# Seven block products instead of eight for w_out in the last three batches, with the relu kept in fp32

## The chip, the cores and the metric

The kernel runs on one core of a Trainium2 chip. The metric is the device time of one execution in microseconds (us). A profile of one execution stands beside it; engines are PE (TensorE; PEld is its weight load), DVE (VectorE), ACT (ScalarE), POOL (GpSimd) and SP (SyncE, which here issues DMAs).

## The reference

Block-sparse attention with a sorting network, then an FFN with a squared relu, for 4 batches, 8 heads, 768 positions of 64 elements:

```python
P = sort_net                                  # (4, 8, 8, 8), normalised by rows and columns, five times
k_sorted = einsum('bhij,bhjcd->bhicd', P, k_b)    # 8 blocks of 96 positions; v likewise
scores = scale * matmul(q_b, k_sb.T)              # inside a block
attn = softmax(scores)
x = matmul(attn, v_sb)  ->  (3072, 512)
h = maximum(x @ w_in, 0)                          # (3072, 2048)
out = (h * h) @ w_out                             # (3072, 512)
```

## The kernel before, in words

The FFN works on groups of 384 tokens, two to a batch. Its input stands transposed in `xT` (128 x 4 x 3072, bf16). An *up* is one of 16 slices of d_ff: four matmuls with 384 columns into a PSUM bank (`hp`, L1010). ACT takes the relu out of the bank into a bf16 tile `h1` (L1018), DVE squares it into `h2` (L1021), which holds the 16 slices of a group. A *down* is one tile of 128 tokens: 16 matmuls of 512 columns into a bank (`op`, L1040) with slices of `h2` as weights and `w_out_bf` as moving operand, in four parts of four. ACT or DVE copies the bank to `ob`, and SP stores it (L989). The last tile of all is done in two pieces of 384 and 128 columns (`last_tile`, L1068). Ups and downs share three banks (`psf`); attention has four banks in two pairs (`p2`) and one of its own (`ps1`).

Attention works on pairs of heads (hp 0 to 3). For batches 2 and 3 its steps are: N and V (`s_nat`, L780) multiply k and v by the sorting matrix on PE, in small tiles of the array; ACT or DVE takes the result out (`kn`, `vn`). Z (`s_turn`) turns k and q: SP issues a DMA transpose from `kn` to `kx` (L835), DVE copies that into `kvT` (L840); DVE copies q into `qi` (L852), and a DMA transpose brings it to `qz` (L862). S (`s_sc`, L695) makes the scores with row-tiled matmuls, ACT the exps (L724). A (`s_av`, L886) averages v, DVE divides (`rec` L896, `ao` L897). X (`s_xt`) turns the result into `xT`, by DMA transpose (L921), or, for hp 3 of batches 0 and 1, by PE (L939) and a copy. q of batch 1 is turned by PE (`s_q`, L574).

The order of the work is set at build time. Each step is recorded with a cost, its engine or engines and what it depends on; `Plan.run` walks through them like a list scheduler and fixes the order on every engine. PE has two queues, attention and FFN, and the table DUES says behind how many FFN pieces an attention step is due. On the chip each engine runs its instructions in that order and waits on semaphores. POOL issues the loads of q, k and v; those of a late batch stand behind a small copy (`held`, L1156) that waits for x^T of the batch before.

Of the kernel before, what the change touches and what calls it, by code (L numbers as in the profile page):

```python
# [8 lines left out]
FP32 = mybir.dt.float32  # L9
# [30 lines left out]
    (2, "A"): (86.0, 88.0, 99.0, 94.5),  # L40
    (2, "X"): (97.5, 103.0, 103.0, 102.0),
    (3, "L"): (109.0,),
    (3, "N"): (111.5, 130.0),
# [4 lines left out]
    (3, "X"): (150.5, 170.0, 236.5, 211.5),
# [5 lines left out]
         "F4 F6 F7 X3")  # L54


class Op:


    def __init__(self, eng, cost, fn, deps, due=0, mode="full"):  # L60
# [47 lines left out]
class Plan:  # L108
# [27 lines left out]
    def run(self):  # L136
# [4 lines left out]
        while att or ffn or rest:  # L141
            best = None
            for op in rest:
# [5 lines left out]
                if best is None or s < best[0][0]:  # L149
                    best = ((s, s + c), op, e, c)  # L150
# [34 lines left out]
def kernel(  # L185
# [92 lines left out]
    kvT_r, et_r, vs_r, qz_r = [], [], [], []  # L278
    for n in range(3):
# [41 lines left out]
    w_t = const.tile([128, NH // 4, 4, NB], BF16)  # L321
    qkv = {}
# [23 lines left out]
    def load(b, t, h0, n, p=slice(0, 128), deps=()):  # L346
        def dst_src():
# [6 lines left out]
            readers[b - 2] + [holds[b]] if b > 1 else list(deps),  # L354
# [90 lines left out]
    tiles = {}  # L445

# [378 lines left out]
    def q_late(z):  # L825
        return qz_r[z % 3][:, z // 3, :, :]
# [390 lines left out]
```

## Time and profile before

| | us |
|---|---|
| median of 3 runs | 217.51 (217.35 to 217.57) |
| span of the profiled execution, first to last instruction | 215.8 |
| what lies outside the span, if that execution took the median | 1.7 |
| PE busy | 209.8 |
| ACT busy | 122.4 |
| DVE busy | 110.0 |
| POOL busy | 27.0 |

The profiled execution's own time is shown by its span alone; its sum with what lies around it is set against the median. In a group's row stand the line, engine and operation, output<-input, shapes and count, then busy us, mean ns of one, and the idle time ahead of them with what ended it. Matmuls are pipelined, so the mean of one is longer than the spacing. A chain row has its start, its length and what ran.

### The profile page before, as it was taken

To read this page: it belongs to the slowest core of one execution; us is meant where nothing else is said; L and a number is where in the kernel's file an instruction comes from. 1 tells how busy PE (TensorE), PEld (TensorE's weight loads), DVE (VectorE), ACT (ScalarE), POOL (GpSimd) and SP (SyncE) were. 2 spreads that over 40 slices of the span, in tenths; PEclk is the share of its full clock that TensorE was granted. 3 is DMA by queue.
4 is the path that set the end of the run, shared out by engine and by line. 5 is a ranking of instruction groups with operands and counts; after the bars stand their busy time and mean duration, and the time that the engine had idled before them with its cause. 6 is when DMAs were issued, how large, how long until landed. Compare 5 with 4: busy or idle time off the path is not lost.

```text
span 215.8 us, 5098 instructions
## 1 busy us (share of the span) xinstructions
PE 209.8 (97%) x2036; PEld 115.7 (54%) x2036; DVE 110.0 (51%) x316; ACT 122.4 (57%) x251; POOL 27.0 (13%) x47
## 2 busy tenths in 40 slices
PE   7899999999999999999999999999999999999994
PEld 2477675446654565445655465445655555455542
DVE  5877677146795446335875047407775154015300
ACT  4787985248765277347774278318874375137421
POOL 7983230000000700000000420000000000000000
PEclk9999999999999999999999999999999999999999
DMA  6999999999978599199994699497988410231012
GB/s 151 216 202 207 207 207 207 191 225 274 185 160 107 94 229 213 24 195 220 169 197 118 114 195 212 90 211 165 163 204 115 103 45 3 49 73 24 0 52 97
DMA packets 47959, 31.91 MB, mean 148 GB/s; under 512 B 27392, under 2 KB 43008, under 8 KB 47936
## 3 DMA queue, kind: packets, MB, share of 16 engines
q1 hardware_dynamic: 35712, 18.35, 41.2%
q0 software_dynamic: 12224, 13.24, 37.1%
q8 instruction: 16, 0.26, 0.5%
q14 instruction: 7, 0.06, 0.1%
HBM read 29.70 MB, written 8.72 MB: 178 GB/s over the span
## 4 chain that ended last, share of the span: by engine, by line
PE 94%; DMA 2%; ACT 1%; issue 1%; DVE 0%; POOLq 0%
PE hp L1010 39%; PE op L1040 37%; PE p L886 4%; PE p L695 4%; DMA qb<-in_q_dram 2%; PE p L451 2%; PE p L780 2%; PE op L1068 2%; PE qtp L574 1%; PE vbp L744 1%; PE tp L624 1%; PE p L660 1%; PE hp L966 0%; PE xtp L939 0%; ACT et L715 0%
## 5 line engine op out<-in xcount | busy, mean ns | idle before, releaser
L1010 PE MATMUL hp<-xT,w_in_bf 128*128 128x384 bf16 x506 | 87.6, 326 | 0.0
L1040 PE MATMUL op<-w_out_bf,h 128*128 128x512 bf16 x368 | 84.9, 379 | 0.0
L1021 DVE TENSOR_TENSOR h<-h 128x384 bf16<-128x384 bf16 x128 | 44.0, 355 | 56.1 <-ACT h L1018 55.5
L1018 ACT ACTIVATE h<-hp 128x384 bf16<-128x384 f32 x128 | 61.8, 495 | 17.6 <-PE hp L1010 14.8
L1010 PEld LDWEIGHTS <-w_in_bf 128*128 128x128 bf16 x506 | 47.7, 98 | 32.2 <-issue 1.1
L1040 PEld LDWEIGHTS <-h 128*128 128x128 bf16 x368 | 33.9, 98 | 37.9 <-issue 1.0
L248 ACT COPY ob<-op 128x512 f32<-128x512 f32 (+2 forms) x25 | 14.2, 569 | 49.0 <-PE op L1040 46.6
L724 ACT ACTIVATE et<-p 96x384 bf16<-96x384 f32 x48 | 19.9, 487 | 6.1 <-PE p L695 6.1
L897 DVE TENSOR_TENSOR ao<-p,rec 96x512 bf16<-96x512 f32 x32 | 22.0, 686 | 1.3 <-DVE rec L896 0.2
L886 PEld LDWEIGHTS <-et 96*128 96x128 bf16 x256 | 11.2, 97 | 5.3 <-issue 0.7
L896 DVE RECIPROCAL rec<-p 96x8 f32<-96x8 f32 x32 | 6.4, 201 | 10.6 <-PE p L886 10.2
L1156 POOL COPY held<-xT 1x3 bf16<-1x3 bf16 (+1 forms) x2 | 0.4, 184 | 84.6 <-DMA xT<-ao 84.6
L250 DVE CAST vn<-p 128x768 bf16<-128x768 f32 x6 | 5.7, 958 | 7.3 <-PE p L780 7.2
L250 DVE CAST kn<-p 128x768 bf16<-128x768 f32 x5 | 4.8, 958 | 9.1 <-PE p L780 9.1
L886 PE MATMUL p<-vblk,et 96*128 96x65 bf16 x192 | 9.4, 193 | 0.0
L451 PE MATMUL p<-ones 128*128 128x512 bf16 (+1 forms) x28 | 8.2, 439 | 1.1 <-DVE ones L274 1.1
L695 PEld LDWEIGHTS <-kvT 64*128 64x128 bf16 x256 | 6.1, 94 | 5.3 <-issue 3.4
L840 DVE COPY kvT<-kx 128x768 bf16<-128x768 bf16 x10 | 8.5, 848 | 0.0
L248 ACT CAST vn<-p 128x768 bf16<-128x768 f32 x6 | 4.8, 797 | 5.8 <-PE p L780 5.8
L330 POOL DMA_DIRECT2D kb<-in_k_dram x10 | 6.5, 649 | 4.4 <-DMA w_in_bf<-in_moe_w_in_dram 1.8
L330 POOL DMA_DIRECT2D vb<-in_v_dram x10 | 6.3, 630 | 3.6 <-DMA w_in_bf<-in_moe_w_in_dram 3.6
L248 ACT CAST kn<-p 128x768 bf16<-128x768 f32 x5 | 4.0, 805 | 4.7 <-PE p L780 4.7
(81 smaller groups left out, 118.2 us busy)
## 6 DMA issues: line engine op xcount, KB each, us to landing
out_dram<-ob SPq DMA_DIRECT2D x20, 256.0 KB, 4.3
v_way<-vn SPq DMA_DIRECT2D x6, 396.0 KB, 5.8
vblk<-v_way SPq DMA_DIRECT2D x6, 396.0 KB, 4.2
vb<-in_v_dram POOLq DMA_DIRECT2D x6, 384.0 KB, 11.7
kb<-in_k_dram POOLq DMA_DIRECT2D x6, 384.0 KB, 10.4
qb<-in_q_dram POOLq DMA_DIRECT2D x6, 384.0 KB, 13.1
w_in_bf<-in_moe_w_in_dram POOLq DMA_DIRECT2D x4, 512.0 KB, 12.5
w_out_bf<-in_moe_w_out_dram POOLq DMA_DIRECT2D x4, 512.0 KB, 17.0
```

Of the source, the lines that this page charges most:

```text
L248: nc.scalar.copy(out=out, in_=in_)
L250: nc.vector.tensor_copy(out=out, in_=in_)
L330: nc.gpsimd.dma_start(out=dst, in_=src)
L451: nc.tensor.matmul(out=p2[slot][:, 0, 0:128 * r].rearrange("p (r x) -> p r x", r=r), lhsT=ones, rhs=ones[:, None, :].to_broadcast([128, r, ...
L695: nc.tensor.matmul(out=scp[:, h, BLK * n:BLK * (n + 1)], lhsT=u.ksT[64 * h:64 * (h + 1), HS * hf + BLK * n:HS * hf + BLK * n + 128], rhs=( ...
L724: nc.scalar.activation(out=et[:, h, 0:HS].rearrange("p (n c a) -> p n c a", c=C0, a=NA), in_=st["p"][0:96, h, 0:HS].rearrange("p (n a c) - ...
L886: nc.tensor.matmul(out=oup[:, h, 66 * n:66 * n + D + 1], lhsT=et_r[u.et[hf]][:, h, BLK * n:BLK * n + 128], rhs=(u.vs[:, NQ * hf + n, h, 0: ...
L897: nc.vector.tensor_tensor(out=u.ao[:, n0:n0 + NQ, :, :].rearrange("p n e d -> p e n d"), in0=ov[:, :, :, 0:D], in1=rec[:, :, :, None].to_b ...
L1010: nc.tensor.matmul(out=t["hp", nt][:, 0:HS], lhsT=w_in_bf[:, kc, 128 * nt:128 * (nt + 1)], rhs=xT[:, kc, t0:t0 + HS], start=(kc == 0), sto ...
L1018: nc.scalar.activation(out=t["h1", nt], in_=t["hp", nt][:, 0:HS], func=AF.Relu)
L1021: nc.vector.tensor_tensor(out=t["h2"][:, nt, :], in0=t["h1", nt], in1=t["h1", nt], op=ALU.mult)
L1040: nc.tensor.matmul(out=t["op", mt], lhsT=t["h2"][:, nt, 128 * mt:128 * (mt + 1)], rhs=w_out_bf[:, nt, :], start=(nt == 0), stop=(nt == NT ...
```

## The change

In batches 1 to 3 the 2048 rows and 512 columns of w_out are cut into 2 x 2 blocks, and so is a pair of row tiles of `h2` (A11, A12 above A21, A22). Where eight block products stood, seven are made, each 8 matmuls of 256 columns (Winograd's form of Strassen's method). Four differences of blocks of w_out (T1 to T4) are made once, by DVE; T1 takes the place of a block of w_out, T2 to T4 stand in batch 1's q, k and v buffers, so that batch 3 loads into batch 2's. Each pair needs four sums of blocks of `h2` (S1 to S4), made by DVE, three of them in place. The products of a pair use two banks: P6 and P7 accumulate on P1, P3 on P5, with an eviction after each (P1s, U2s, P5s are kept in fp32; the sums go into `ob`). Ups use all banks that are free, from a pool of four (`Banks`). A batch has three pairs: the first is woven into the ups of the second group, the other two alternate behind them.

The relu is written in fp32, and a square takes two slices at once, on DVE or ACT; the h1 ring has four slots. The k copy and the q copy may go to ACT too. For hp 3 of batches 2 and 3, q is turned by PE through a bank of `p2`, and x^T likewise. Among steps that can start at the same time the planner now prefers evictions, then relus, then squares. The table DUES has other numbers. The split of the last tile by columns falls away; of the last pair the lower row tile is stored in halves. Batch 0's FFN keeps the bf16 relu and the plain downs.

```diff
-    (2, "L"): (40.0,),
+    (2, "L"): (34.5,),
...
+Q_PE = {2: (3,), 3: (3,)}
+X_PE = {1: (3,), 2: (3,), 3: (3,)}
+PRIO = {"evict": -3, "relu": -2, "square": -1, "sum": 0.5}
...
-                if best is None or s < best[0][0]:
+                if best is None or (s, op.prio) < (best[0][0], best[1].prio):
...
-    r1, r2, rf, rh1, rh2, rob = Ring(1), Ring(2), Ring(3), Ring(3), Ring(2), Ring(4)
+    r1, r2, rf, rh1, rh2, rob = Ring(1), Ring(2), Ring(3), Ring(4), Ring(2), Ring(4)
...
-            readers[b - 2] + [holds[b]] if b > 1 else list(deps),
+            readers[0 if b == 2 else 2] + [holds[b]] if b > 1 else list(deps),
...
-        u.k_op = plan.add("DVE", 0.87, k_blocks, [k_op] + u.old)
+        u.k_op = plan.add(AD, (0.85, 0.87), k_blocks, [k_op] + u.old)
...
+        if hp in Q_PE.get(b, ()):
+            slot, old = r2.take()
+            def q_mm(e):
+                qb = qkv[b][0]
+                for a in range(NA):
+                    for h in range(2):
+                        nc.tensor.transpose(
+                            out=first_bank(slot, (NA, 128))[64 * h:64 * (h + 1), a, :],
+                            in_=qb[:, 2 * hp + h, D * a:D * (a + 1)], identity=ident)
...
+            pe = plan.add("PE", 0.334, q_mm, [landed[b, 0, HP * (2 * hp // HP), 0]] + old, due,
+                          mode="col")
+            readers[b].append(pe)
+            u.q_op = plan.add(AD, cost_b(S), q_ev, [pe] + rq3)
+            rq3[:] = [u.q_op]
+            u.qT = qT_r[3]
+            return
...
-        qp = plan.add("DVE", 0.4, q_pair, [landed[b, 0, HP * (2 * hp // HP), 0]] + oldi)
+        qp = plan.add(AD, (0.85, 0.4), q_pair, [landed[b, 0, HP * (2 * hp // HP), 0]] + oldi)
...
-        if early or u.b > 1 or u.b == 1 and u.hp < HP - 1:
+        if early or u.b > 0 and u.hp not in X_PE[u.b]:
...
-        ring = r1 if own else rf
+        ring = r2 if u.b > 1 else r1 if own else rf
...
+    h1_r = const.tile([128, 4, HS], FP32)
...
+    NH2, DH = NT // 2, d_model // 2
+    B11, B12 = w_out_bf[:, 0:NH2, 0:DH], w_out_bf[:, 0:NH2, DH:]
+    B21, B22 = w_out_bf[:, NH2:, 0:DH], w_out_bf[:, NH2:, DH:]
+    T1 = B12
+    T2, T3, T4 = (t[:, 0:NH2 * DH].rearrange("p (j m) -> p j m", m=DH) for t in qkv_r[1])
+    s3_r = [t[:, NH2 * DH:NH2 * DH + NH2 * 128].rearrange("p (j x) -> p j x", x=128)
+            for t in qkv_r[1]]
+    keep_r = ([t.rearrange("p a x -> p (a x)")[:, 0:2 * DH].bitcast(FP32) for t in qT_r[0:3]]
+              + [t[:, 1, 0:2 * DH].bitcast(FP32) for t in kvT_r])
+    def make_t():
+        deps = readers[1] + [landed["w_out", part] for part in range(4)]
+        def add(name, dst, x, y, deps):
+            tsum[name] = []
+            for j in (slice(0, NH2 // 2), slice(NH2 // 2, NH2)):
+                tsum[name].append(plan.add(
+                    "DVE", 0.68, lambda e, j=j: nc.vector.tensor_tensor(
+                        out=dst[:, j, :], in0=x[:, j, :], in1=y[:, j, :], op=ALU.subtract), deps))
+        add("T3", T3, B22, B12, deps)
+        add("T1", T1, B12, B11, deps + tsum["T3"] + plain)
+        add("T2", T2, B22, T1, deps + tsum["T1"])
+        add("T4", T4, B21, T2, deps + tsum["T2"])
...
+        def up(self, nt):
+            n, old = fb.take()
+            s1, old1 = rh1.take()
...
+            pe = plan.add("PE", 0.65, mm, self.xs + [landed["w_in", nt // 4]] + old, ffn=True)
+            r = plan.add("ACT", cost_f(HS)[0], lambda e: nc.scalar.activation(
+                out=h1_r[:, s1, :], in_=banks[n][:, 0:HS], func=AF.Relu), [pe] + old1)
+            r.prio = PRIO["relu"]
+            fb.use(n, pe, r)
+            fb.release(n)
+            if nt % 2:
+                (sa, ra), (sb, rb) = self.relus[-2:]
+                h1 = h1_r[:, sa:sa + 2, :]
+                h2 = self.h2[:, nt - 1:nt + 1, :]
+                def square(e):
+                    if e == "ACT":
+                        nc.scalar.activation(out=h2, in_=h1, func=AF.Square)
+                    else:
+                        nc.vector.tensor_tensor(out=h2, in0=h1, in1=h1, op=ALU.mult)
+                op = plan.add(AD, (0.9, 0.95), square, [ra, rb] + self.old2)
+                op.prio = PRIO["square"]
+                self.sq += [op, op]
...
+            A11, A12 = g1.h2[:, 0:NH2, x1], g1.h2[:, NH2:, x1]
+            A21, A22 = g2.h2[:, 0:NH2, x2], g2.h2[:, NH2:, x2]
+            self.s3 = add(S3, A11, A21, ALU.subtract, self.hi1 + self.hi2 + olds + readers[1])
+            self.s1 = add(A21, A21, A22, ALU.add, [self.s3] + g2.sq)
...
+        def product(self, a, b, n, deps, start):
+            def mm(e):
+                for j in range(NH2):
+                    nc.tensor.matmul(out=banks[n][:, 0:DH], lhsT=a[:, j, :], rhs=b[:, j, :],
+                                     start=(start and j == 0), stop=(j == NH2 - 1), skip_group_check=not start)
+            pe = plan.add("PE", 0.875, mm, deps, ffn=True)
+            fb.use(n, pe)
...
+        def evict(self, n, dst, deps, other=None):
+            src = banks[n][:, 0:DH]
+            if other is None:
+                op = plan.add(AD, cost_f(DH), lambda e: copy(e, dst, src), deps)
+            else:
+                op = plan.add("DVE", cost_f(DH)[1], lambda e: nc.vector.tensor_tensor(
+                    out=dst, in0=src, in1=other, op=ALU.add), deps)
...
+        def step(self, k):
+            A11, A12, A21, A22, S3 = self.S
+            o = self.ops
+            if k == 1:
+                self.a, old = fb.take()
+                o[1] = self.product(A11, B11, self.a, self.hi1 + old, True)
+                self.p1 = self.evict(self.a, self.P1s, [o[1]] + self.oldk + plain)
+                self.s2 = self.add(A11, A21, A11, ALU.subtract, [self.s1, self.s3, o[1]])
+            elif k == 2:
+                self.b, old = fb.take()
+                o[2] = self.product(A12, B21, self.b, self.gs[0].sq + old, True)
+                self.c11 = self.evict(self.b, ob_r[self.o1][:, top], [o[2], self.p1] + self.oldo[1],
+                                      self.P1s)
+                self.s4 = self.add(A12, A12, A11, ALU.subtract, [self.s2, o[2]])
+            elif k == 5:
+                o[5] = self.product(A21, T1, self.b, [self.s1, self.c11] + tsum["T1"], True)
+                self.p5 = self.evict(self.b, self.P5s, [o[5]] + self.oldk)
+            elif k == 6:
+                o[6] = self.product(A11, T2, self.a, [self.s2, self.p1] + tsum["T2"], False)
+                self.u2 = self.evict(self.a, self.U2s, [o[6]] + self.oldk)
+            elif k == 3:
+                o[3] = self.product(A12, B22, self.b, [self.s4, self.p5], False)
+                self.c12 = self.evict(self.b, ob_r[self.o1][:, low], [o[3], self.u2], self.U2s)
+                fb.release(self.b)
+                rkeep.use(self.nk, self.c12)
+                self.put(self.o1, self.row1, [self.c11, self.c12], ())
+            elif k == 7:
+                o[7] = self.product(S3, T3, self.a, [self.s3, self.u2] + tsum["T3"], False)
+                rs3.use(self.ns, o[7])
+                self.c22 = self.evict(self.a, ob_r[self.o2][:, low], [o[7], self.p5] + self.oldo[2],
+                                      self.P5s)
+                rkeep.use(self.nk, self.c22)
+            else:
+                o[4] = self.product(A22, T4, self.a, [self.c22] + tsum["T4"], False)
+                self.c21 = self.evict(self.a, ob_r[self.o2][:, top], [o[4]])
+                fb.release(self.a)
+                self.put(self.o2, self.row2, [self.c22, self.c21], (low, top))
...
+        def put(self, so, row, ops, halves):
+            dst = out[row:row + 128, :]
+            if self.last and halves:
+                for x, op in zip(halves, ops):
+                    store(so, dst[:, x], ob_r[so][:, x], [op])
+            else:
+                store(so, dst, ob_r[so], ops)
...
+    def ffn_batch(b):
+        g1, g2 = Group(2 * b), Group(2 * b + 1)
+        for nt in range(NT):
+            g1.up(nt)
+        nt = 0
+        for k in (None, 1, 2, 5, 6, 3, 7, 4, None):
+            for _ in range(3 if nt == 0 else 2):
+                if nt < NT:
+                    g2.up(nt)
+                    nt += 1
+            if k == 1:
+                p = Pair((g1, 0), (g1, 1))
+            if k:
+                p.step(k)
+        ps = [Pair((g1, 2), (g2, 0)), Pair((g2, 1), (g2, 2), b == B - 1)]
+        for k in "1A 2A 1B 2B 5A 6A 5B 6B 3A 7A 3B 7B 4A 4B".split():
+            ps[k[1] == "B"].step(int(k[0]))
...
-        holds[b] = plan.add("POOL", 0.1, hold, [x_done[b - 1, x, 0] for x in range(HP - (b == 2))])
+        holds[b] = plan.add("POOL", 0.1, hold, [x_done[b - 1, x, 0] for x in range(HP - 1)])
...
+    for g in range(2):
         ffn_unit(g)
+    make_t()
+    for b in range(1, B):
+        ffn_batch(b)
```

Three places in the order. ACT's queue around the first step of N or V in batch 1's first group (L1018 is the relu, L248 a copy out of PSUM). Before:

```order
L1018 ACTIVATE h1_1677<-hp_1660 128x384
L248 CAST vn0_113<-p2_0_78 128x6x2x64
L1018 ACTIVATE h1_1699<-hp_1687 128x384
L1018 ACTIVATE h1_1708<-hp_1694 128x384
L1018 ACTIVATE h1_1717<-hp_1702 128x384
L248 CAST kn2_121<-p2_0_78 128x768
L248 COPY ob_1756<-op_1711 128x512
```

and now, in the same place (L1176 is the relu, L1191 a square, L267 a copy out of PSUM):

```order
L1176 ACTIVATE h1_r_163<-bank2_73 128x384
L267 CAST kn2_120<-p2_0_69 128x768
L1176 ACTIVATE h1_r_163<-bank0_71 128x384
L267 CAST kn3_121<-p2_1_70 128x768
L1176 ACTIVATE h1_r_163<-bank1_72 128x384
L1176 ACTIVATE h1_r_163<-bank3_74 128x384
L1191 ACTIVATE h2_0_164<-h1_r_163 128x768
L1176 ACTIVATE h1_r_163<-bank2_73 128x384
```

N now comes ahead of V and earlier in the group, a square of two slices stands between the relus, and the banks go round by four.

The end of the program: before, DVE ends with squares and ACT with the relus and these evictions of the last downs:

```order
L1018 ACTIVATE h1_3195<-hp_3181 128x384
L248 COPY ob_3215<-op_3189 128x512
L248 COPY ob_3235<-op_3210 128x512
L248 COPY ob_3255<-op_3230 128x384
L248 COPY ob_3270<-op_3250 128x128
```

Now DVE ends with the sums and evictions of the last two pairs (L1217 a sum, L1248 an eviction with an addition):

```order
L1217 TENSOR_TENSOR h2_1_165<-h2_1_165 128x8x128 x2
L1248 TENSOR_TENSOR ob0_166<-bank2_73,kvT0_88 128x256
L1217 TENSOR_TENSOR h2_0_164<-h2_1_165,h2_0_164 128x8x128
L1217 TENSOR_TENSOR h2_1_165<-h2_1_165 128x8x128
L1217 TENSOR_TENSOR h2_0_164<-h2_0_164 128x8x128
L1248 TENSOR_TENSOR ob2_168<-bank1_72,qT0_84 128x256
L1217 TENSOR_TENSOR h2_1_165<-h2_1_165 128x8x128
L1248 TENSOR_TENSOR ob0_166<-bank2_73,kvT1_96 128x256
```

S1 of both pairs, P2's eviction of the first, S2 of both, S4, P2's eviction of the second, S4, P3's eviction: the products wait for them in turn.

SP's queue in batch 3 before, the last turns of q and of x^T (`xT`) with stores between:

```order
L862 DMA_TRANSPOSE qz2_110<-qi0_123 128x6x128
L835 DMA_TRANSPOSE kx0_127<-kn0_119 128x6x128
L862 DMA_TRANSPOSE qz0_94<-qi1_124 128x6x128
L921 DMA_TRANSPOSE xT_82<-ao_2586 128x8x96
L810 DMA vblk2_118<-v_way 96x2112
L989 DMA out_0_dram<-ob_2450 128x512
L989 DMA out_0_dram<-ob_2475 128x512
L921 DMA_TRANSPOSE xT_82<-ao_2718 128x8x96
```

and now:

```order
L864 DMA_TRANSPOSE kx0_126<-kn0_118 128x6x128
L915 DMA_TRANSPOSE qz1_101<-qi3_125 128x6x128
L1036 DMA out_0_dram<-ob0_166 128x512
L1036 DMA out_0_dram<-ob1_167 128x512
L832 DMA vblk2_117<-v_way 96x2112
L974 DMA_TRANSPOSE xT_77<-ao_2554 128x8x96
```

Three turns of q and three of x^T are left in the queue for the batch where four stood; the stores of the woven pair come ahead of the x^T turns and of the read of `vblk2`.

More of the change, by code (lines that the diff above doesn't have):

```diff
@@ L278 @@
     kvT_r, et_r, vs_r, qz_r = [], [], [], []
+    qT_r = [const.tile([128, NA, 128], BF16, name=f"qT{n}") for n in range(4)]
     for n in range(3):
@@ L1054, in ffn_unit @@
-        if g == n_tok // HS - 1:
-            last_tile(t, sq, t0 + HS - 128)
-    def last_tile(t, sq, row):
-        W = 3 * d_model // 4
-        for half, cols in enumerate((slice(0, W), slice(W, d_model))):
-            n = cols.stop - cols.start
-            sf, old = rf.take()
-            for part in range(4):
-                def down(e, half=half, cols=cols, part=part, n=n):
-                    if part == 0:
-                        t["op", half] = psf.tile([128, d_model], FP32, tag="pf", name="op")
-                    for nt in range(4 * part, 4 * part + 4):
-                        nc.tensor.matmul(
-                            out=t["op", half][:, 0:n],
-                            lhsT=t["h2"][:, nt, HS - 128:HS],
-                            rhs=w_out_bf[:, nt, cols],
-                            start=(nt == 0), stop=(nt == NT - 1))
-                pe = plan.add("PE", 0.65 if half == 0 else 0.25, down, sq[4 * part:4 * part + 4] + old, ffn=True)
-                old = []
-            rf.use(sf, put(("op", half), t, n, out[row:row + 128, cols], pe, None), pe)
+                plain.append(pe)
@@ new lines, in ffn_unit @@
+            so, old = rob.take()
+            op = plan.add(AD, cost_f(d_model), lambda e, so=so, sf=sf: copy(e, ob_r[so], banks[sf]),
+                          [pe] + old)
+            rf.use(sf, pe, op)
+            store(so, out[t0 + 128 * mt:t0 + 128 * (mt + 1), :], ob_r[so], [op])
+    plain = []
+    NH2, DH = NT // 2, d_model // 2
[3 more added lines that the diff above has]
+    T2, T3, T4 = (t[:, 0:NH2 * DH].rearrange("p (j m) -> p j m", m=DH) for t in qkv_r[1])
@@ new lines, with __init__, take, use @@
+    class Banks:
+        def __init__(self, order):
+            self.free = list(order)
+        def take(self):
+            n = self.free.pop(0)
+            ring, i = (r1, 0) if n == 3 else (rf, n)
+            old, ring.users[i] = ring.users[i], []
+            return n, old
+        def use(self, n, *ops):
+            ring, i = (r1, 0) if n == 3 else (rf, n)
+            ring.users[i] += ops
+            ring.all[i] += ops
+        def release(self, n):
+            self.free.append(n)
@@ L1173 @@
         stage(int(due))
-    for g in range(n_tok // HS):
+    for g in range(2):
         ffn_unit(g)
+    t = rf.turn
+    fb = Banks(((t + 1) % 3, (t + 2) % 3, 3, t))
+    make_t()
+    for b in range(1, B):
+        ffn_batch(b)
     started = filled = False
```

241 lines of the change are left out of this document (147 added, 94 removed).

## The prediction

> **What bounds the kernel now.** I read the page first, then the chain that ended last, then windows by stage, then the groups by form.
>
> ```profile
> span 215.8 us, 5098 instructions
> PE 209.8 (97%) x2036; PEld 115.7 (54%) x2036; DVE 110.0 (51%) x316; ACT 122.4 (57%) x251; POOL 27.0 (13%) x47
> PEclk9999999999999999999999999999999999999999
> ```
>
> PE is busy for 97% of the span at the full granted clock. Busy alone proves little, so the chain follows (start, us, what):
>
> ```profile
> 48.67 0.46 PE qtp L574 x12
> ...
> 73.40 0.34 PE xtp L939 x8
> ...
> 75.47 8.45 PE hp L1010 x52
> 83.92 0.31 PE p L780 x16
> ...
> 108.34 0.65 PE hp L1010 x4
> 108.99 0.25 PE p L886 x8
> 109.24 0.65 PE hp L1010 x4
> 109.89 0.28 PE p L695 x8
> 110.17 0.76 PE hp L1010 x4
> ...
> 149.87 0.45 PE p L695 x16
> ...
> 171.09 10.40 PE hp L1010 x64
> 181.50 10.36 PE op L1040 x48
> ...
> 202.25 6.91 PE op L1040 x32
> 209.16 3.51 PE op L1068 x32
> 212.67 0.02 issue
> 212.69 0.27 ACT ob L248
> ```
>
> From 75.47, where batch 1's FFN begins, to 212.67 the chain is PE without a gap: 137.2 us. An up product (4 matmuls of 384 columns) takes 10.40/16 = 0.65; a 512-column matmul 10.36/48 = 0.2158. So time here is what PE has to issue, plus any wait that the change makes. The only surcharge is a change of array tiling: the up group at 110.17, behind the row-tiled scores (L695), takes 0.76 instead of the 0.65 at 108.34, so 0.11 for a change.
>
> The other engines have room now (stretch; then PE, PEld, DVE, ACT, POOL busy, clock, DMA):
>
> ```profile
> 145.56:171.09 25.53, 25.53 (x257) 14.20 (x256) 15.59 (x37) 15.74 (x36) 0.00 (x0) 1.00 0.86 159
> ```
>
> With attention and FFN mixed, ACT and DVE are each busy 61 to 62%.
>
> Durations for the sum (busy us, mean ns):
>
> ```profile
> L1018 ACT ACTIVATE h<-hp 128x384 bf16<-128x384 f32 x128 | 61.8, 495 | 17.6 <-PE hp L1010 14.8 <-DVE h L1021 1.1
> L1021 DVE TENSOR_TENSOR h<-h 128x384 bf16<-128x384 bf16 x128 | 44.0, 355 | 56.1 <-ACT h L1018 55.5
> L897 DVE TENSOR_TENSOR ao<-p,rec 96x512 bf16<-96x512 f32 x32 | 22.0, 686 | 1.3 <-DVE rec L896 0.2
> L724 ACT ACTIVATE et<-p 96x384 bf16<-96x384 f32 x48 | 19.9, 487 | 6.1 <-PE p L695 6.1
> L248 ACT COPY ob<-op 128x512 f32<-128x512 f32 x23 | 13.5, 586 | 46.6 <-PE op L1040 46.6
> L840 DVE COPY kvT<-kx 128x768 bf16<-128x768 bf16 x10 | 8.5, 848 | 0.0
> L896 DVE RECIPROCAL rec<-p 96x8 f32<-96x8 f32 x32 | 6.4, 201 | 10.6 <-PE p L886 10.2
> L250 DVE CAST vn<-p 128x768 bf16<-128x768 f32 x6 | 5.7, 958 | 7.3 <-PE p L780 7.2
> L1068 PEld LDWEIGHTS <-h 128*128 128x128 bf16 x32 | 2.5, 98 | 1.3
> L250 DVE CAST kvT<-tp 128x384 bf16<-128x384 f32 x3 | 1.7, 553 | 0.1
> L472 ACT CAST qb<-xT 128x768 bf16<-128x768 f32 x2 | 1.6, 822 | 0.3 <-DMA xT<-in_q_dram 0.3
> L426 DVE TENSOR_TENSOR p_sb<-p_sb,rs 32x64 f32<-32x64 f32 x5 | 1.1, 212 | 0.2
> L500 DVE TENSOR_TENSOR w_all<-mask,pt 128x256 bf16<-128x256 bf16 x2 | 0.8, 419 | 0.0
> L374 DVE TENSOR_TENSOR fold<-ident 128x64 bf16<-128x64 bf16 x1 | 0.2, 172 | 0.0
> L248 ACT COPY ob<-op 128x128 f32<-128x128 f32 x1 | 0.3, 266 | 0.4 <-PE op L1068 0.4
> ```
>
> **The change, part by part, on PE.** Removed in batches 1 to 3: 18 row tiles of 16 matmuls. Seventeen at 16 x 0.2158 are 58.7, the last (L1068) 3.5: 62.2 us. Added: 9 pairs x 7 products x 8 = 504 matmuls of 256 columns. No row has that width as a dense stream; L1068 brackets it. Its 16 matmuls of 384 columns take 2.60, so the 16 of 128 columns 0.91, 0.057 each; halfway lies 0.110, half of a 512 is 0.108. I take 0.1095: 55.2 us (ends 54.4 and 55.4). Net -7.0.
>
> Added: two q turns of 12 transposes, 0.46 as at 48.67 with the change into the tiling, 0.11 out of it: 1.1. Two x^T turns as at 73.40: 0.7. The new order has 45 changes of tiling from batch 1's first up product on where 36 stood; four belong to the q turns, five more cost 0.6. Two more before that: 0.2. PE in sum: -7.0 + 1.1 + 0.7 + 0.6 + 0.2 = -4.4 us. The four DMA transposes that go from SP's queue were hidden behind ups; they are worth nothing.
>
> **The tail.** The last eviction has 256 columns, by ACT's rows for 128 and 512 columns 0.37 instead of 0.27. The last store doubles:
>
> ```profile
> out_dram<-ob SPq DMA_DIRECT2D x7, 64.0 KB, 1.6
> out_dram<-ob SPq DMA_DIRECT2D x1, 192.0 KB, 1.9
> ```
>
> 128 KB lies between: 0 to 0.3, I take 0.2. Together +0.3.
>
> **New waits on PE** are the open term; before there were none in this stretch. The relus write fp32, a square takes two of them at once (768 elements, fp32 in) on ACT or DVE. On ACT 0.82 (L472, the same shape from SBUF). On DVE one element per cycle: 0.212 for 64 elements (L426), and 1.05 ns per element between L250's 384 and 768, so 0.95 where two bf16 squares took 0.71. A sum of 1024 bf16 elements: from L374's 64 and L1021's 384 0.57 ns per element, 0.72. An eviction of 256 columns with its addition on DVE 0.42 (L250 less 128 elements), a plain one on ACT 0.37.
>
> ACT is the tightest in batch 1, from its first up product to its last. PE issues there 32 ups (20.8), 6 products (5.25), four pieces of N and V as at 83.92 (1.2), two units' scores as at 149.87 (0.9), the q turn (0.35) and 16 changes (1.8): 30.3 us. ACT gets 32 relus (15.8), 8 squares (6.6), 8 exps (3.9), 3 kn casts (2.4), 2 qi (1.6), 2 kvT copies (1.7), 2 product evictions (0.7) and one ob (0.6): 33.4 us in 58 instructions. By mean durations ACT is short by 3.1, and PE is held since a relu frees the bank that an up needs next; behind a late relu stand the exps and kvT copies of the same queue, for which PE's averages and scores wait. The same count gives 30.7 on 29.4 in batch 2 and 24.8 on 26.0 in batch 3, so PE waits 4.4 us in sum if ACT really takes its durations. But back to back they overlap:
>
> ```profile
> 61.15 0.49 ACT L1018 ACTIVATE h<-hp 128x384 bf16<-128x384 f32 x1 [0.16 <-PE hp L1010]
> 61.54 0.86 ACT L724 ACTIVATE et<-p 96x384 bf16<-96x384 f32 x2
> ...
> 84.34 0.79 ACT L248 CAST vn<-p 128x768 bf16<-128x768 f32 x1
> 85.03 1.14 ACT L1018 ACTIVATE h<-hp 128x384 bf16<-128x384 f32 x2
> ```
>
> The exp starts 0.39 after a relu of 0.49, the relu 0.69 after a cast of 0.79: 0.10 saved each. 58 x 0.10 = 5.8 leaves 27.6 on 30.3. Then ACT fits, at 91%, where it now has 62%.
>
> DVE is fullest under batch 1's last 15 products (16.8 us on PE with batch 2's scores and averages between): 8 rec and ao (7.1), 6 sums (4.3), 6 evictions (2.5), x^T's copy (0.6): 14.5. In batch 3 no attention stands between the last products. After the last up ends: its result 0.16 later (326 ns for a matmul that is issued every 162), relu 0.50, ACT's square 0.82, then on DVE two sums, an eviction, three sums, an eviction: 1.5 + 1.44 + 0.42 + 2.16 + 0.42 = 5.9. The product that waits for that eviction stands seven products on, at 6.1. It just fits.
>
> So waits lie between 0 and 4.4; the overlap rows are the nearest, and I take 1.0 for places where a square or an exp stands ahead of a relu whose bank PE needs: the pair of row tiles holds two of the four banks, so an up waits for the relu two ups back. With two ups and a product (2.2 us) to a turn that relu has 1.5 us from its up's end to the next use of its bank, and needs 0.16 + 0.50; one square ahead of it (0.72 with the overlap) still fits, a square and an exp don't.
>
> The sum: 217.5 - 4.4 + 0.3 + 1.0 = 214.4 us (span 212.7; 1.7 us lie outside the span).
>
> T's 8 sums (5.8 us of DVE) cost nothing: they lie under batch 0's last and batch 1's first ups, where ACT squares meanwhile; without ACT's squares the fifth relu would wait for six of these sums (4.3), while four ups cover 2.6: 1.7 us. Batch 3's loads are issued by POOL behind the same event as before, the x^T transposes of batch 2 (now three of them, the fourth goes through PE), and reuse batch 2's buffer, whose readers stand ahead of that event anyway. An eviction into an ob buffer waits for its store of four tiles before; with 256 KB stores as before and 2.2 us and more between them I cost this at nothing, and the cover is SP's queue not being held by a transpose that waits for a norm; if it is, the eviction and with it the next product in that bank are late by what the norm is late.
>
> **Rivals.** (1) ACT does not overlap where squares and relus alternate, since a square needs the relu just ahead: waits 4.4, so 217.8 less what the banks buffer (an up's length, 0.65): 217.2, no change. For it: 91% load in a fixed order. Against: the overlap rows.
>
> (2) Slower: DVE's sums run at one element per cycle. They read slices of h2, and L500, bf16 with a broadcast view, shows such a rate: 0.419 for 256, so 1.22 for 1024. Place: the last products of each batch. In batch 3 five sums more at 0.5 move the eviction from 5.9 to 8.4 where PE wants it at 6.1: 2.3; with as much in batches 1 and 2, 7 us: 221. It decides from 0.5 us more per batch than I allow, about 0.95 per sum: beyond, 3.3 us are gone. Against: runs of 128 adjacent elements, unlike the broadcast.
>
> (3) The saving does not come, because weight loads no longer hide: 504 loads of 98 ns where 288 were. 216 x 0.098 = +21 us: 235. Against: L1068's matmuls of 128 columns are spaced 57 ns with loads of 98 ns, so loads overlap there. The Trainium skill (TensorE: Matmul & The Clock Gate, Part 3, the list of what overlaps) says a weight load overlaps running matmuls only where the row group differs; all row groups are the same here, and the trace contradicts it.
>
> **How the numbers follow.** Waits of 0 to 2 (213.0 to 215.6): 0.72. Rival 1 and what lies up to it: 0.14. Rival 2 in part or whole: 0.11. Rival 3: 0.01; 0.02 for what I don't see. A range to 217.4 takes in most of rival 1. 0.2%, 0.4 us, is about what this measurement can tell from no change. Faster: 0.72 and half of rival 1, 0.79; same 0.07; slower 0.14.
>
> **What would show it.** PE product groups at 0.11 a matmul; PE busy about 4 us less; PE's waits on relus and evictions 1 us in sum; DVE sums of 0.72, squares of 0.95, ACT squares of 0.82. Product matmuls over 0.12, sums over 0.95, or ACT gapless while PE waits would make it wrong.

## The result, and the profile after

The changed kernel takes 216.25 us (median; 215.87 to 219.28) where the kernel before takes 217.51. The ratio is 0.9942 with a 95% interval of 0.9923 to 0.9962: faster, by 0.6%, as the forecast said by its sign, but by 1.26 us and not by 3.1. Ratios here leave out executions in which the chip was disturbed, so they can differ a little from the ratio of two medians.

The page of the changed kernel, in its lines on the span and the engines:

```profile
span 216.5 us, 5592 instructions
PE 208.1 (96%) x2271; PEld 138.1 (64%) x2276; DVE 130.2 (60%) x307; ACT 151.8 (70%) x302; POOL 27.1 (13%) x47
```

PE is busy 1.7 us less (3.2 us less in the later execution named next, at 206.6, which has the same order on every engine); ACT is now at 70% and DVE at 60%. The span is longer than the 215.8 before, although the time is shorter: this execution, of 218.37 us, began badly. The matmuls on `ones` that keep PE going at the start were slow in it, here beside the same matmuls in a later execution (the bf16 run below):

```profile
6.98 4.12 PE L475 MATMUL p<-ones 128*128 128x512 bf16 x12
...
6.55 2.66 PE L475 MATMUL p<-ones 128*128 128x512 bf16 x12
```

So the first up product stands at 24.28 here, at 22.23 there and at 22.21 before. As the order is the same there, the late start doesn't come from the order of the change, and I compare spans from the first up product on: 215.8 - 22.21 = 193.59 before, 216.5 - 24.28 = 192.22 after, -1.37 us, which is what the medians say.

The chain of the changed kernel, at its stage borders (first up 24.28, batch 1 from 78.56, batch 2 from 126.25, batch 3 from 173.70) and where it leaves PE:

```profile
24.28 1.08 PE bank L1056 x6
...
57.59 0.77 ACT et L747 x2
...
78.56 5.20 PE bank L1169 x32
...
99.59 0.38 ACT h_r L1176
...
100.23 0.83 ACT kvT L267
...
105.42 0.53 PE p L885 x12
...
126.25 7.15 PE bank L1169 x44
...
156.93 1.51 ACT kvT L267
...
173.70 13.65 PE bank L1169 x84
...
199.74 13.20 PE bank L1234 x120
212.96 0.37 ACT ob L267
```

Where the chain before was PE without a gap, ACT now carries it in three places: at 57.6 to 61.6 (exps of batch 1, under group 1's ups), at 98 to 105 and at 156 to 160. In the last two stands the copy of k into its blocks, `kvT`, and nothing like it stood on ACT before. Batch 3 is PE alone again. PE's own waits (us in sum, times, longest) are small in the list:

```profile
PE p L885 <- ACT et L747: 0.8, 1, 0.8
PE bank L1056 <- ACT h_r L1063: 0.6, 1, 0.6
PE p L939 <- ACT et L747: 0.3, 1, 0.3
PE bank L1080 <- issue: 0.3, 2, 0.2
```

The groups by form that answer to the durations of the forecast:

```profile
L267 ACT COPY kvT<-kx 128x768 bf16<-128x768 bf16 x5 | 8.0, 1607 | 0.0
L269 DVE COPY kvT<-kx 128x768 bf16<-128x768 bf16 x5 | 4.2, 868 | 0.0
L1193 DVE TENSOR_TENSOR h<-h_r 128x768 bf16<-128x768 f32 x19 | 18.1, 957 | 23.5 <-ACT h_r L1176 23.5
L1191 ACT ACTIVATE h<-h_r 128x768 bf16<-128x768 f32 x29 | 24.5, 845 | 0.8
L1217 DVE TENSOR_TENSOR h<-h 128x1024 bf16<-128x1024 bf16 x24 | 16.0, 684 | 0.5 <-ACT h L1191 0.4
L1248 DVE TENSOR_TENSOR ob<-bank,qT 128x256 f32<-128x256 f32 x15 | 6.3, 420 | 9.6 <-PE bank L1234 8.0 <-ACT h L1191 1.3 <-ACT qT L267 0.3
```

Squares (0.957, 0.845), sums (0.684) and evictions (0.420) came out as estimated. One row did not: the block copy of k, at which the forecast counted 0.85 us on ACT, takes 1.607 there. Five of the ten copies are on ACT.

The borders of the kernel before that the forecast didn't show:

```profile
22.21 1.08 PE hp L1010 x6
...
123.54 7.15 PE hp L1010 x44
```

By stretches, us:

| | before | after | after, straight copies on ACT | corrected cost, new due times |
|---|---|---|---|---|
| first up product to batch 1's first | 53.26 | 54.28 | 54.29 | 53.54 |
| batch 1 | 48.07 | 47.69 | 46.80 | 47.08 |
| batch 2 | 47.55 | 47.45 | 46.87 | 47.08 |
| batch 3, to the last eviction | 41.60 | 39.26 | 39.26 | 39.26 |
| last eviction to the end | 3.11 | 3.54 | 3.47 | 3.61 |
| sum | 193.59 | 192.22 | 190.69 | 190.57 |

The last two columns are experiments, told next.

### The profile page after: what moved, and what is told of

Same layout as the page of the kernel before. It is cut to its first block, busy times and chain, and to the rows that moved or that the text cites. A ratio compares the mean times of both kernels' runs of the same rounds, so it can differ in the third digit from the quotient of the medians.

```text
span 216.5 us, 5592 instructions
## 1 busy us (share of the span) xinstructions
PE 208.1 (96%) x2271; PEld 138.1 (64%) x2276; DVE 130.2 (60%) x307; ACT 151.8 (70%) x302; POOL 27.1 (13%) x47
## 4 chain that ended last, share of the span: by engine, by line
PE 87%; ACT 7%; DMA 2%; issue 2%; DVE 0%; POOLq 0%
PE bank L1169 28%; PE bank L1234 23%; PE bank L1080 10%; PE bank L1056 8%; PE p L939 4%; PE p L716 3%; PE p L475 2%; DMA qb<-in_q_dram 2%; ACT et L747 2%; PE p L802 2%; ACT kvT L267 1%; PE bank L595 1%; ACT h_r L1176 1%; PE bank L766 1%; PE p L678 1%
## 5 line engine op out<-in xcount | busy, mean ns | idle before, releaser
L1169 PE MATMUL bank<-xT,w_in_bf 128*128 128x384 bf16 x384 | 67.4, 327 | 0.0
L1176 ACT ACTIVATE h_r<-bank 128x384 f32<-128x384 f32 x96 | 44.3, 490 | 7.0 <-PE bank L1169 5.6
L1234 PEld LDWEIGHTS <-h 128*128 128x128 bf16 x432 | 40.8, 98 | 7.0 <-issue 0.2
L1234 PE MATMUL bank<-w_out_bf,h 128*128 128x256 bf16 x288 | 36.1, 273 | 0.0
L1193 DVE TENSOR_TENSOR h<-h_r 128x768 bf16<-128x768 f32 x19 | 18.1, 957 | 23.5 <-ACT h_r L1176 23.5
L1191 ACT ACTIVATE h<-h_r 128x768 bf16<-128x768 f32 x29 | 24.5, 845 | 0.8
L267 ACT COPY ob<-bank 128x256 f32<-128x256 f32 (+1 forms) x13 | 6.1, 470 | 25.5 <-PE bank L1234 14.0
L1056 PE MATMUL bank<-xT,w_in_bf 128*128 128x384 bf16 x122 | 22.5, 327 | 0.6 <-ACT h_r L1063 0.6
L1080 PE MATMUL bank<-w_out_bf,h 128*128 128x512 bf16 x91 | 21.8, 379 | 0.5 <-issue 0.3
L1063 ACT ACTIVATE h_r<-bank 128x384 bf16<-128x384 f32 x32 | 15.2, 493 | 4.4 <-PE bank L1056 3.9
L1217 DVE TENSOR_TENSOR h<-h 128x1024 bf16<-128x1024 bf16 x24 | 16.0, 684 | 0.5 <-ACT h L1191 0.4
L1066 DVE TENSOR_TENSOR h<-h_r 128x384 bf16<-128x384 bf16 x32 | 10.8, 353 | 7.3 <-ACT h_r L1063 7.3
L1080 PEld LDWEIGHTS <-h 128*128 128x128 bf16 x96 | 8.7, 98 | 9.4 <-issue 0.3
L267 ACT COPY qT<-bank 128x256 f32<-128x256 f32 (+2 forms) x22 | 9.2, 429 | 7.3 <-PE bank L1234 4.7
L1248 DVE TENSOR_TENSOR ob<-bank,qT 128x256 f32<-128x256 f32 x15 | 6.3, 420 | 9.6 <-PE bank L1234 8.0
```

Source lines behind the costliest of these rows:

```text
L267: nc.scalar.copy(out=out, in_=in_)
L1056: nc.tensor.matmul(out=banks[sf][:, 0:HS], lhsT=w_in_bf[:, kc, 128 * nt:128 * (nt + 1)], rhs=xT[:, kc, t0:t0 + HS], start=(kc == 0), stop= ...
L1080: nc.tensor.matmul(out=banks[sf], lhsT=h2[:, nt, 128 * mt:128 * (mt + 1)], rhs=w_out_bf[:, nt, :], start=(nt == 0), stop=(nt == NT - 1))
L1169: nc.tensor.matmul(out=banks[n][:, 0:HS], lhsT=w_in_bf[:, kc, 128 * nt:128 * (nt + 1)], rhs=xT[:, kc, t0:t0 + HS], start=(kc == 0), stop=( ...
L1176: r = plan.add("ACT", cost_f(HS)[0], lambda e: nc.scalar.activation(out=h1_r[:, s1, :], in_=banks[n][:, 0:HS], func=AF.Relu), [pe] + old1)
L1191: nc.scalar.activation(out=h2, in_=h1, func=AF.Square)
```

## The experiments

Theory A: the seven products save what was reckoned, and the copies of k on ACT, twice as long as counted, give it back by holding the relus, exps and turned q behind them. Theory B: the early wait, eight exps of batch 1 among group 1's ups. Theory C, the rival, is the first rival of the forecast: ACT is simply too full, and whatever is taken from it, PE waits.

**Straight copies.** The order stays, only ACT's five copies read kx without the strides.

```diff
+            n = 1 if e == "ACT" else NB
-            copy(e, u.ksT[:, 0:S].rearrange("p (n x) -> p n x", n=NB),
-                 kx_r[kx].rearrange("p (x n) -> p n x", n=NB))
+            copy(e, u.ksT[:, 0:S].rearrange("p (n x) -> p n x", n=n), kx_r[kx].rearrange("p (x n) -> p n x", n=n))
```

> The changed kernel with the same order of instructions; only where ACT copies the turned k (kx to kvT, five times, in batches 1 and 2) it reads kx straight through instead of in its strided block order (so k's blocks of those five units lie in another order). Theory A (five strided copies at 1.607 us each, where 0.85 was counted, hold the relus that PE waits for): the copies fall to about 0.82, the waits of PE of 0.81 at 104.6 and 0.34 at 159.9 go, 215.1 us. Theory C (ACT is simply too full with relus, squares and exps; the copy is only the last in line): the copies get shorter, but at least 0.8 of the 1.15 us of waits stays, 215.9 or more.

214.72 us, ratio 0.9862 (0.9814 to 0.9909). Its group row, the waits of PE from the first up on, and the chain at batch 1's start and at the end:

```profile
L267 ACT COPY kvT<-kx 128x768 bf16<-128x768 bf16 x5 | 4.2, 833 | 0.0
...
PE bank L1056 <- ACT h_r L1063: 0.6, 1, 0.6
PE bank L1080 <- issue: 0.3, 2, 0.2
...
76.50 5.20 PE bank L1169 x32
...
209.43 0.37 ACT ob L267
```

A copy falls to 0.833, both waits of batches 1 and 2 are gone, and those two batches are 0.89 + 0.58 = 1.47 us shorter; no other stretch moved by more than 0.07. That is nearly the whole difference of the medians (1.53). ACT still has all relus, squares and exps, and none of the waits of batches 1 and 2 is left where theory C asked for at least 0.8 of them: it is out.

**All copies on DVE**, as in the kernel before, by `plan.add("DVE", 0.87, k_blocks, ...)`.

> The changed kernel with all block copies of k on DVE, as in the kernel before; the order on the engines follows from that. Theory A: ACT loses 8.0 us, DVE gains 4.3 and has room for them; the waits at 104.6 and 159.9 go: 215.1 to 215.4 us. Theory C: ACT's other work keeps the waits, or DVE gets late with sums and squares: 216.0 or more.

216.72 us, ratio 0.9943 (0.9914 to 0.9972); 192.52 from the first up. The waits of batches 1 and 2 gave way to new ones:

```profile
PE p L716 <- DVE ao L950: 1.1, 1, 1.1
PE p L939 <- ACT et L747: 0.5, 1, 0.5
```

The first lies in batch 1: a copy of 0.87 more stands in DVE's queue between the divisions (`ao`) and the sums of the last pairs, and the scores wait for the bank pair that `ao` frees. So taking the copy from ACT is not enough while the due times were chosen with it there. My expectation of 215.1 to 215.4 was wrong.

**The early scores later**, with `(1, "S"): (-30.0, -46.0, -14.0, 16.0)` for `(-40.5, ...)`.

> The changed kernel with the scores of batch 1's first pair of heads moved from under group 1's ups to its w_out product, so that four exps instead of eight stand among the relus. Theory B (the eight exps keep back the relus whose banks the ups need; PE idles 0.85 us between 49.8 and 78.6): that idle time falls under 0.2, 215.4 us. Rival (the exps wait only elsewhere: under the w_out product the averages wait for them): the idle time stays at 0.7 or more, 216.0 to 216.5.

218.3 us, ratio 0.9997 (0.9961 to 1.0033), 194.86 us from the first up: 2.6 worse than the change. The wait on the relu is gone, others came, and behind them the chain has a product of 8 matmuls that takes 1.82 us where 0.88 is usual:

```profile
PE p L716 <- DVE ao L950: 1.1, 3, 0.5
PE p L939 <- DVE ao L950: 0.8, 2, 0.4
...
117.66 1.82 PE bank L1234 x8
```

The stretch ahead of batch 1 gets no shorter (54.47 us for 54.28). The loss lies in batch 1 (50.64 for 47.69): there DVE's divisions hold PE for 1.7 us, and then the granted clock falls, to 0.83, 0.50 and 0.82 in the three windows of 2 us from 116 on. The lower clock is about 1.7 of the 2.6 us, by the lengths of the chain's pieces there (an estimate). Two of the twelve executions had a granted clock of 0.999, and they took 216.28 and 216.30 us, as long as the change. So theory B's 215.4 did not come; the rival's 216.0 to 216.5 fits these two alone, and its reason, that the averages wait for the exps, was not what held PE.

**Plain products**: the change without seven products and fp32 relu.

```diff
-    t = rf.turn
-    fb = Banks(((t + 1) % 3, (t + 2) % 3, 3, t))
-    make_t()
-    for b in range(1, B):
-        ffn_batch(b)
+    for g in range(2, n_tok // HS):
+        ffn_unit(g)
```

> The changed kernel with plain row tiles of 16 matmuls of 512 columns in batches 1 to 3, bf16 relus and single squares as in batch 0, and no sums of w_out: everything of the change but the seven products and the fp32 relu. If the products give what their rows say (55.2 for 62.2), PE gets 7.0 more and at most loses the waits of 1.15: 221.5 to 223 us, 4 to 5.5 us above the kernel before, which is what the rest of the change costs (q and x^T turns 1.7, averaging and tiling 1.3, the early waits 0.85, tail). If the products gave less than 7.0 (their loads or sums slow something that the rows hide), it is under 220.5.

222.18 us, ratio 1.0188 (1.0139 to 1.0237), inside the forecast 221.5 to 223. Its chain runs from the first up to the last eviction:

```profile
22.45 1.08 PE bank L1056 x6
...
216.36 0.59 ACT ob L267
```

Its span is 220.4, so 197.95 from the first up: the products are worth 5.73 us net, 7.0 of PE's work less the waits of about 1.5 in batches 1 to 3, which plain products don't have. The rest of the change, alone, costs 4.4 us against the kernel before.

**Strides on the writing side**: ACT reads kx straight and writes kvT in strides.

```diff
-            copy(e, u.ksT[:, 0:S].rearrange("p (n x) -> p n x", n=NB),
-                 kx_r[kx].rearrange("p (x n) -> p n x", n=NB))
+            v = "p (n x) -> p x n" if e == "ACT" else "p (n x) -> p n x"
+            copy(e, u.ksT[:, 0:S].rearrange(v, n=NB), kx_r[kx].rearrange("p (x n) -> " + v[-5:], n=NB))
```

> The changed kernel in the same order; ACT's five block copies of k read kx straight through and write kvT in strides, so that the result is the same as before the edit. If only strided reading makes ACT slow, a copy takes about 0.82 instead of 1.607, PE's waits in batches 1 and 2 go as with the straight copy (214.72): 214.7 us. If ACT is as slow in writing in strides, a copy stays at 1.6 and the time at 216.2.

230.53 us, ratio 1.0543 (1.0485 to 1.0602). Neither expectation was right; it is far worse:

```profile
L267 ACT COPY kvT<-kx 128x768 bf16<-128x768 bf16 x5 | 20.1, 4027 | 0.0
...
PE p L716 <- ACT kvT L267: 4.7, 2, 2.4
PE p L939 <- ACT et L747: 4.0, 3, 2.2
```

2.4 us more in each of five copies make 12.1, and the kernel becomes 14.3 us slower than the change; from 0.833 to 1.607 the five copies grew by 3.9 and cost 1.5. So ACT's slack in these stretches ends between the two, and most of what goes beyond it is passed on. Not all of the 14.3 is ACT's delay, though: behind the long waits the granted clock falls to 0.50, at 108 to 110 and again at 122 to 124. By the clock in the windows of 2 us that is about 3 us (an estimate).

**Half exps**: `HS >> (u.b == 1 and u.hp < 2)` as the width in both operands of the exp.

> The changed kernel in the same order; the exps of batch 1's first two pairs of heads do half of their columns (the other half is left as it was). Theory B (the eight exps of 0.4 to 0.5 us, among group 1's relus, make PE idle 0.85 us): each is 0.16 to 0.2 us shorter, 1.4 us in sum, the idle time before 62 falls under 0.2, 215.4 to 215.7 us. Rival (the stretch from batch 0's first up to batch 1's is 1.0 us longer for its other changes of order, more tiling changes and later averages): the stretch stays at 54.0 or more, 216.0 us.

216.5 us, ratio 0.9941 (0.9919 to 0.9963), the same as the change. The exps fall to 0.326 and the stretch from 54.28 to 53.97, 0.31 us of the 1.02 it had gained. Theory B as I put it, that 0.85 us come back with the eight exps, fell; a wait of 0.3 on the relu stays. What makes up the rest was not traced; that another order can win most of it is seen below, at the new due times.

**q and x^T by DMA again**: `Q_PE = {}` and `X_PE = {1: (3,), 2: (), 3: ()}`. The x^T turns that the edit gives back to the DMA are those of batches 2 and 3, not of 1 and 2 as the expectation has it.

> The changed kernel with q and x^T of the last pairs of batches 2 and 3 (x^T of batches 1 and 2) turned by DMA again. As cost alone the turns are 1.05 + 0.68 us of PE: 214.5 us. Rival (they pay for themselves: the last pair's transposed x comes too late by DMA, with 1.2 us for the transpose and 2 to 3 us to landing, and PE stands before the next batch's first up, twice): 216.5 to 219 us.

223.25 us, ratio 1.023 (1.019 to 1.0271), worse than the rival's 216.5 to 219. The wait, the chain at batch 2's start, and the granted clock in 40 slices of the span:

```profile
PE bank L1169 <- DMA xT<-ao: 3.1, 2, 2.5
...
124.31 5.32 DMA xT<-ao
...
129.67 7.20 PE bank L1169 x33
...
PEclk9999999999999999999999979999999999999999
```

The next batch's first up waits for the last transposed x, and behind the wait the granted clock is 0.50 for 2 us: the 33 matmuls take 7.20 us where at the usual 0.1625 they take 5.36, so 1.8 us go to the clock beside the 3.1 of the wait. From the first up it takes 221.6 - 23.73 = 197.87 us: the turns that cost 1.6 us of PE are worth 5.6 net in this order.

**bf16 relus in batches 1 to 3**, with `.bitcast(BF16)` on `h1_r`, in the same order.

> The changed kernel in the same order; the relus of batches 1 to 3 write bf16, so that a square reads bf16 (as in the kernel before). DVE's 19 squares fall from 0.957 to about 0.62, ACT's 29 stay at about 0.83. If DVE is not on the path, the fp32 relu costs nothing: 216.0 to 216.4 us. If the sums that wait for squares hold the products at the ends of the batches, 0.3 to 1 us comes back: 215.2 to 215.9.

216.27 us, ratio 0.9948 (0.9914 to 0.9981), 192.17 from the first up against 192.22: no difference.

```profile
L1193 DVE TENSOR_TENSOR h<-h_r 128x768 bf16<-128x768 bf16 x19 | 10.6, 557 | 26.9 <-ACT h_r L1176 26.8
```

19 x 0.40 = 7.6 us of DVE are saved and nothing comes of it; the fp32 relu is free here.

**The true price in the planner**, and due times chosen anew with it (a few of the table's lines):

```diff
-        u.k_op = plan.add(AD, (0.85, 0.87), k_blocks, [k_op] + u.old)
+        u.k_op = plan.add(AD, (1.6, 0.87), k_blocks, [k_op] + u.old)
...
-    (1, "S"): (-40.5, -46.0, -14.0, 16.0),
+    (1, "S"): (-46.0, -69.5, -45.0, 2.5),
...
-    (2, "S"): (59.0, 63.5, 68.5, 81.5),
+    (2, "S"): (61.0, 62.5, 67.0, 87.0),
...
-    (3, "A"): (134.0, 143.0, 154.5, 158.5),
+    (3, "A"): (134.5, 150.0, 155.0, 159.0),
```

> The changed kernel with the measured 1.6 instead of 0.85 as the planner's cost of a block copy on ACT, and the due times of the attention steps of batches 1 to 3 chosen anew with it. The planner then puts all ten copies on DVE. Theory A (the wrong price of this copy made the waits, and nothing in the seven products themselves): waits of PE under 0.8 us in sum from the first up on, 214.0 to 214.7 us. Theory C (ACT and DVE are too full for any order): as with the copies simply on DVE, waits of 2 us, 216 to 217.

214.55 us (214.29 to 215.23), ratio 0.9856 (0.9818 to 0.9894): 1.4% faster than the kernel before, and its interval lies wholly below that of the change. The list of PE's waits from the first up on is empty. Its chain at the same borders:

```profile
21.93 1.08 PE bank L1056 x6
...
75.47 7.80 PE bank L1169 x48
...
122.55 13.65 PE bank L1169 x84
...
169.63 13.65 PE bank L1169 x84
...
208.89 0.37 ACT ob L267
```

All ten copies are on DVE, as in the run above that gained nothing; here the order was chosen for it. It also wins 0.74 us back in the stretch before batch 1. Theory A's forecast came true, but two things changed at once, the price and the search for due times: a new choice of due times with the old price was not tried, so how much of the gain belongs to the price alone is not shown. This is the best version that I have timed.

**Copies on POOL**, by `plan.add("POOL", 1.6, k_blocks, ...)` and `nc.gpsimd.tensor_copy`.

> The changed kernel with all ten block copies of k on POOL, which has nothing to do in batches 1 to 3 but to issue loads. Theory A: if POOL needs 2 us or less for a copy and doesn't slow DVE, ACT loses 8.0 us and DVE 4.2, PE's waits in batches 1 and 2 go: 214.5 to 215.0 us. If POOL needs 3 us or more, the scores wait for it twice a batch: 217 or more.

215.81 us in 6 runs that lie wide apart (213.94 to 217.41), ratio 0.9892 (0.9837 to 0.9947). In the profiled execution PE has no wait of 0.3 us or more behind batch 1's first up, and it takes 215.3 - 24.83 = 190.47 from the first up on. Why its runs spread more than the others' is open; the profiled one (217.1) began as badly as that of the change, with 4.33 us for the matmuls on `ones`. POOL's copies, and what DVE's sums became beside them:

```profile
L869 POOL COPY kvT<-kx 128x768 bf16<-128x768 bf16 x10 | 17.6, 1764 | 69.8 <-DMA kx<-kn 66.7 <-PE p L716 2.0 <-PE p L802 1.1
...
L1217 DVE TENSOR_TENSOR h<-h 128x1024 bf16<-128x1024 bf16 x24 | 17.6, 749 | 0.4 <-ACT h L1191 0.2
L1217 DVE TENSOR_TENSOR kb<-h,h 128x1024 bf16<-128x1024 bf16 x3 | 3.4, 1117 | 1.9 <-ACT h L1191 1.9
```

**No copies**: the scores load their weights from kx in its strides.

```diff
-                            lhsT=u.ksT[64 * h:64 * (h + 1), HS * hf + BLK * n:HS * hf + BLK * n + 128],
+                            lhsT=(kx_r[u.kx].rearrange("p (x n) -> p n x", n=NB)[64 * h:64 * (h + 1), NQ * hf + n, :]
+                                  if hasattr(u, "kx") else u.ksT[64 * h:64 * (h + 1), HS * hf + BLK * n:HS * hf + BLK * n + 128]),
...
-        u.k_op = plan.add(AD, (0.85, 0.87), k_blocks, [k_op] + u.old)
+        u.k_op = k_op
+        u.kx = kx
```

> The changed kernel without block copies of k: the scores' weight loads read the turned k in its strided order, 96 columns instead of 128. If a strided load costs about the 94 ns of a plain one, ACT loses 8.0 and DVE 4.2 us and PE waits 1 us less: 214.7 to 215.5 us. If it costs several times as much, 160 loads come into the open: at 0.4 us each up to 50 us more.

225.76 us, ratio 1.0367 (1.0325 to 1.0408). A strided load takes 266 ns where a plain one takes 94:

```profile
L716 PEld LDWEIGHTS <-kx 64*96 64x96 bf16 x160 | 15.1, 266 | 3.1 <-issue 3.1
L716 PEld LDWEIGHTS <-kvT 64*128 64x128 bf16 x96 | 2.3, 94 | 1.4 <-issue 0.6 <-DVE qi L269 0.3
```

No wait of PE lies behind this: PE itself is busy for 216.6 us. So these loads come into the open, and that costs 9.5 us against the change. The load has 96 columns here and 128 there, so stride and width are not parted; a plain load of 64 columns takes 110 ns in the changed kernel (L642), which leaves most of the 266 to the stride if 96 columns lie near these two.

## Why the prediction was right or wrong, step by step

Sums by line along PE's chain give each term; the run with straight copies has all of PE in batches 1 to 3 on its chain, so it is set against the kernel before.

| term | forecast | measured | from |
|---|---|---|---|
| 504 product matmuls for the row tiles | -7.0 | -7.04 | 56.07 for 63.11 |
| q turns | +1.1 | +0.92 | straight copies |
| x^T turns | +0.7 | +0.68 | straight copies |
| changes of tiling | +0.6 | +1.2 | N and V 3.46 for 2.48, scores 3.96 for 3.85, ups 63.61 for 63.51 |
| batch 0's part | +0.2 | +1.02 | 54.28 for 53.26 |
| waits in batches 1 to 3 | +1.0 | +1.47 | after less straight copies |
| tail | +0.3 | +0.43 | 3.54 for 3.11 |
| sum | -3.1 | -1.3 | |

**The products** are right to 0.04 us, 0.111 a matmul with the tiling changes around them against 0.1095. The third rival, weight loads that no longer hide, would have shown here: PEld has 22.4 us more and the products none.

**Changes of tiling** were undersized by 0.6 us. I counted changes; nearly all of the cost is in V. The four N steps still take 0.31 us each, but the two pieces of 8 matmuls in each of the four V steps no longer run as one: a piece by itself takes 0.28 to 0.29 where the 16 took 0.31, and a step takes 0.51 to 0.58.

**Batch 0's part** is the largest miss by size, 0.82 us. I let the attention of batch 1 that moves ahead cost two changes of tiling, and did not ask what its exps do to the relus of batch 0: the count of ACT's load was made only from batch 1 on, where I looked for the tightest place. With the new due times the stretch takes 53.54, so another order wins 0.74 of the 1.02 back; half exps recover 0.31. That the eight exps alone cause it is not shown.

**Waits** is the failed step that matters most, because it is the one that the experiments turn on and off: 1.5 us of the time hang on it. Its form was right: ACT at its limit in batch 1, its queue holding what PE needs. The wrong number is in the list of ACT's work, "2 kvT copies (1.7)": 0.85 was DVE's row (L840), and the same copy on ACT takes 1.607. Put right, the two copies make ACT's sum in batch 1 1.5 us longer: 29.1 on PE's 30.3, by the forecast's own count with the overlap. By that sum ACT would still fit; the wait of 0.8 comes where two copies, exps and relus stand close together in its queue (98 to 105), which a sum over a batch can't show. With straight copies, at the durations I had counted, batches 1 to 3 wait for nothing at all, and the kernel takes 214.72 where I said 214.4. So the overlap and with it the case against rival 1 (waits of 4.4 by ACT's mean durations) hold; the 1.0 that I allowed was for other waits, which did not come, and hid most of the mistake. That the term looks only 0.5 off is luck. The row that should have warned me was in the trace of before: 848 ns for a bf16 copy of 768 elements on DVE, while q's copy of the same shape, in runs of 64 elements, takes DVE 352 ns:

```profile
L852 DVE COPY qi<-qb 128x768 bf16<-128x768 bf16 x10 | 3.2, 352 | 0.0
```

The copy was slow for its pattern, and what that pattern costs on ACT no row showed: an unknown cost, for which I took one value without bounds.

**Squares, sums, evictions, fp32 relu, T's sums** are right, and cost nothing as said; rival 2 (sums at one element a cycle) is refuted by 0.684.

**DMA transposes "worth nothing"** holds for the kernel before. In the new order it isn't so: with them the kernel is 5.6 us longer, 1.8 of it by the lower clock behind the wait. The sum was not touched by it.

**The tail** took 0.43 for 0.3: an eviction of 0.37 and the 128 KB store.

So the direction came from the products and held, and 1.8 us of the forecast gain are missing: 0.8 ahead of batch 1, 0.6 in the changes of tiling, 0.5 in the waits, 0.1 in the tail, less 0.2 at the turns. The copies alone are 1.5 of it by experiment: without their strides the change gives 190.69 - 193.59 = -2.9 us.

## What to carry to other kernels

When an operation may move to another engine, price it there with its access pattern, not with the row of the engine it leaves; a copy that is slow for its strides is the first to bound from both sides. When a planner sets the order, correct the price there and choose the order anew: so done, the same work with all copies on DVE waited for nothing, while moving the copy by hand and keeping the due times gained nothing. A wait of PE can cost more than its length, since in three runs the granted clock fell behind it. And where work is moved ahead, count the load of the engine that it lands on in the stretch it goes to as well.

## What the runs showed of the hardware

The price of strides, in this kernel's copy of 768 bf16 elements a partition: on ACT 0.833 us straight, 1.607 with reads 16 bytes apart, 4.027 with writes 192 bytes apart; on DVE 0.868 and on POOL 1.764 with the strided reads; for TensorE a load of 96 columns with the same strides 266 ns, where a plain one of 128 takes 94. Writes were tried at 192 bytes alone and reads at 16, so whether ACT is slower by the writing or by the wider step is not shown. The Trainium skill (SBUF — State Buffer, Door 1: The DMA port swizzle, the note on cachelines there) says that SBUF has lines of 16 bytes and that each access that crosses to a new one pays. The strided read touches one element in each line, and the runs agree in that it is slow, on ACT and in the weight loads; how much each engine pays is from these runs alone.

DVE's sums beside POOL's copies: of the 27 in the two rows above, three began while a POOL copy ran (at 96.67, 144.60 and 146.43 us), and they took 1.78, 1.14 and 1.97 us, each ending about 0.55 us behind the copy. In the changed kernel the same two rows have means of 0.684 and 0.694. The Trainium skill (SBUF — State Buffer, Who interferes with whom) says that a DVE instruction with two inputs from SBUF contends with a GpSimd instruction that reads SBUF. The trace agrees. From the first up on, the profiled execution was still as short as that of DVE with its new order (190.47 us against 190.57), though the medians are 215.81 and 214.55.

The granted clock fell to 0.50 in three runs, each time behind a stretch in which PE had stood for a good part: with the early scores later, PE was busy 2.28 of 4 us at 114 to 118, and the clock was 0.50 at 118 to 120; with the turns by DMA, 1.53 of 4 us at 126 to 130, and 0.50 at 130 to 132; with strides on the writing side, 0.99 of 4 us at 104 to 108, and 0.50 at 108 to 110. With all copies on DVE PE was busy 0.93 of 2 us at 116 to 118, and the clock stayed at 1.00. How long PE must stand for the clock to fall these runs don't say.
